# First requests for w_in at 120 partitions each, the last 8 partitions by a request of their own

## The chip, the cores and the metric

One Trainium2 chip; the kernel runs on one of its cores. The metric is the device time of one execution in microseconds, the median of several runs. Before the change it is 368.2 us, median of 3 runs (367.98 to 368.25).

## The reference

Two blocks in a row. The first is a gated linear attention that steps through the sequence (4 batches, 8 heads, 768 steps, head size 48); its output is laid out as 3072 tokens by 384 columns. The second multiplies the tokens by w_in (384 x 1024), applies a softmax-weighted unit with a layer norm, and multiplies by w_out (1024 x 384):

```python
for t in range(S):
    state = alpha[:, :, t, :, None] * state + np.einsum('bhd,bhe->bhde', k[:, :, t], v[:, :, t])
    y[:, :, t] = np.einsum('bhd,bhde->bhe', q[:, :, t], state)
...
h = x @ w_in
e = np.exp(h - np.max(h, axis=-1, keepdims=True))
solu = h * e / (np.sum(e, axis=-1, keepdims=True) + 1e-09)
mu = np.mean(solu, axis=-1, keepdims=True)
var = np.mean((solu - mu) ** 2, axis=-1, keepdims=True)
return ((solu - mu) / np.sqrt(var + 1e-06) * g_ln) @ w_out
```

The inputs are float32, except w_in and w_out: they are float32 arrays times a double, and so reach the kernel as 64-bit floats.

## The kernel before, in words

The sequence is worked in six groups of 128 steps (G = 6), each for all four batches (B = 4), so a group is 512 tokens. For each group the attention is computed in chunk form: decay scans on VectorE (DVE), scores and outputs on TensorE (PE), masks on DVE; then `up` multiplies the tokens by w_in in eight slices of 128 columns (f = 0 to 7, each three matmuls over the 384 rows, which the profile shows as six records) and `down` multiplies by w_out. The order of instructions is written out by hand (`tc.manual_schedule()`): every engine works through its instructions in program order. For group 0 that order is plain code (from line 668 on), for the later groups a table of steps.

The weights come as 64-bit floats and are made into float32 on the chip. There are eight pieces, `pieces`: numbers 0 to 3 are w_in, 256 of its 1024 columns each, numbers 4 to 7 are w_out, 256 of its 1024 rows each. `fetch(i, slot, n)` (line 567) asks for piece i, or for n pieces that follow each other in one go, into a slot of the tile `room`. A w_in piece is requested in three DMA requests, one for each block of 128 rows of w_in (KC = 3): partition p takes row p of the block, 2 KB of it (4 KB with n = 2). `bit(i, k)` (L616 to L630) are five DVE instructions that turn the raw words in `room` into float32 in w_in or w_out; `in_range(i)` (L598 and L601) are two ScalarE (ACT) instructions that read the same words and note whether any is out of range.

What the change and the steps around it touch, in program order:

- SyncE (SP) issues the loads: alpha, k, q (`load_first`), v (`load_v`, L176), then `fetch(0, 3)`, `fetch(1, 4)` and `fetch(2, 1, 2)` at L578: nine requests for w_in, of 256 KB each for pieces 0 and 1 and 512 KB for pieces 2 and 3 together. The next request of SP is that of `fetch(4, 3)` for w_out; it needs slot 3 again, so it waits until piece 0 has been read by L628 and L598.
- Each request signals its end on a semaphore. Eight semaphores are used in turn for all requests of SP and ACT (numbers 101 and 104 to 110 in the trace), and a request waits until the one eight before it has landed.
- DVE: the last masks of the scores (`masked`, L289), then `bits(0)`, the copy `g_col` (L642), `bits(1)`, and then the steps of pieces 2 to 7, spread over the eight slices of group 0 between the products of L409.
- PE: `read_values` (L333), `keys_back` (L303), then `up_mm` (L394). Its h(0) and h(1) need piece 0, h(2) and h(3) piece 1, h(4) and h(5) piece 2, h(6) and h(7) piece 3. h has two PSUM buffers, so h(f) also waits until ACT (L408) and DVE (L409) have read h(f - 2).
- ACT: `keys_back`'s copies, `in_range(0)`, and for each slice the exponential (L408), a step of `in_range` for a later piece (for f = 0 the first of piece 2) and the square (L412).

At the end each engine reads a flag and branches past a general path that isn't taken (L1422); after that SP waits for the eight DMA semaphores one after the other, and all engines meet (L1449).

Of the kernel before, what the change touches and what calls it, by code (L numbers as in the profile page):

```python
# [11 lines left out]
U32 = mybir.dt.uint32  # L12
# [4 lines left out]
P = 128  # L17
# [15 lines left out]
def fast_path(ctx, tc, q, k, v, alpha, moe_w_in, moe_w_out, moe_g_ln, out):  # L33
# [12 lines left out]
    nc = tc.nc  # L46
# [8 lines left out]
    KC = DM // P  # L55
# [117 lines left out]
    def load_v(g):  # L173
        t = slice(g * P, (g + 1) * P)
        for b in range(B):
            nc.sync.dma_start(out=held(vn, b), in_=v[b, :, t, :].rearrange("h p d -> p h d"))  # L176
# [147 lines left out]
    parts = []  # L324
# [231 lines left out]
    float64 = moe_w_in.dtype != FP  # L556
# [7 lines left out]

    raws = {}

    def fetch(i, slot, n=1):

        kind, f = pieces[i]
        w = n * F // (2 if kind else KC)  # L570
        raw = room[:, 1536 * slot : 1536 * (slot + n)].bitcast(U32).rearrange("p (c f w) -> p c f w", f=w, w=2)
        if kind:
            parts = [(slice(0, P), c, moe_w_out[(f + c) * P : (f + c + 1) * P, :]) for c in range(2)]
        else:
            parts = [(slice(0, P), c, moe_w_in[c * P : (c + 1) * P, f * P : f * P + w]) for c in range(KC)]
        for rows, c, src in parts:
            if float64:
                nc.sync.dma_start(out=raw[rows, c].rearrange("p f w -> p (f w)"), in_=src.bitcast(U32))  # L578
            else:
                dst = w_out[rows, f + c, 0:DM] if kind else w_in[rows, c, f * P : f * P + w]  # L580
                nc.sync.dma_start(out=dst, in_=src)
        for m in range(n):
            raws[i + m] = raw[:, :, w // n * m : w // n * (m + 1)]
# [100 lines left out]
    nc.gpsimd.memset(state, 0.0)  # L684
    nc.gpsimd.memset(kg, 0.0)
    load_v(0)
    fetch(0, 3)
    fetch(1, 4)
    fetch(2, 1, 2)
    nc.vector.memset(ones, 1.0)  # L690
    nc.vector.memset(small_ones, 1.0 / 32)
    nc.vector.memset(mhalf, -0.5)
# [24 lines left out]
    for i in (0, 2, 1):  # L717
        if i == 1:
# [3 lines left out]
            out=qe[:, :, 0:P] if i == 2 else qv[:, part, 0:P], in0=t[i], in1=aT[:, part, 1:SW], op=ALU.mult  # L722
# [199 lines left out]
    for g in range(1, G + 1):  # L922
# [10 lines left out]
        for s in range(FC):  # L933
# [18 lines left out]
            if todo:  # L952
                n, half = todo.pop(0)
# [18 lines left out]
    parts = [N * 3, G * 2, G * NB] + [len(pieces)] * 2  # L972
# [5 lines left out]
    def compare(out, x, bound, op):  # L978
# [6 lines left out]
        out=chunks[:, :, 2], in0=sums[:, :, 2], scalar=0.25, in1=sums[:, :, 3], op0=ALU.mult, op1=ALU.is_le  # L985
# [6 lines left out]
    else:  # L992
# [9 lines left out]
        out=bad, in0=all_ok[0:1, 0:1], scalar1=float(P * ends[-1]), scalar2=None, op0=ALU.is_lt  # L1002
# [415 lines left out]
def kernel(tc, *args):  # L1418

    with ExitStack() as ctx:  # L1420
        taken = fast_path(ctx, tc, *args)
    with tc.If(taken > 0):  # L1422
        general_path(tc, *args)
# [30 lines left out]
```

## Time and profile before

| what | value |
|---|---|
| median of 3 runs | 368.2 us (367.98 to 368.25) |
| the profiled execution's own time | 367.97 us |
| its span, first to last instruction | 366.2 us |
| PE busy | 357.8 us (98%) |
| DVE, ACT, POOL busy | 245.0, 146.4, 132.2 us |
| granted TensorE clock | 1.00 |
| w_in requests: count, KB each, us to landing | 6 of 256 KB, 6.1; 3 of 512 KB, 8.0 |

A line of the profile's timeline gives the start in us, how long, the engine (a q marks its sequencer, as for DMA issues), the line of the kernel, the operation, what it writes and reads, the shape and how many were merged; square brackets give idle time of the engine before it and what ended it. The profile is one execution; 367.97 less 366.2 us lie around its span.

### The profile page before, as it was taken

The numbers are of one execution on the slowest core, as the hardware profiler recorded it, in microseconds if no ns is written. First come the engines' busy times: TensorE is split into PE (matmuls) and PEld (weight loads), VectorE is DVE, ScalarE is ACT, GpSimd is POOL, SyncE is SP. The second block draws the span as 40 slices with busy tenths as digits, with TensorE's granted clock in tenths as the row PEclk, the third lists the DMA queues.
The fourth block names the chain that finished last, engine by engine and source line by source line (L and its number), as shares of the span: only waits on it lengthen the run. The fifth ranks groups of instructions, "written<-read, shape, count | busy, mean of one in ns | idle before, by whom it ended". The sixth has DMA issues, their size and how long they took to land. (4 is left out here: it accounts for less than half of the span.)

```text
span 366.2 us, 10036 instructions
## 1 busy us (share of the span) xinstructions
PE 357.8 (98%) x4341; PEld 215.0 (59%) x4341; DVE 245.0 (67%) x375; ACT 146.4 (40%) x260; POOL 132.2 (36%) x129
## 2 busy tenths in 40 slices
PE   8899999999999999999999999999999999999994
PEld 8784355666755566566575456475556565555552
DVE  0999989979998797936675935766946314345420
ACT  3647878182645262252521252431241132222110
POOL 7020000004449963774133764232773121233300
PEclk9999999999999999999999999999999999999999
DMA  9995995326196409463035354004041000000011
GB/s 180 183 338 152 204 309 124 88 67 159 50 234 141 109 21 180 85 152 94 21 92 112 83 121 126 3 25 88 21 107 55 0 25 0 24 21 22 23 47 51
DMA packets 72871, 36.06 MB, mean 98 GB/s; under 512 B 48232, under 2 KB 70000, under 8 KB 72816
## 3 DMA queue, kind: packets, MB, share of 16 engines
q1 hardware_dynamic: 71792, 34.39, 39.8%
q10 hardware_dynamic: 1024, 0.92, 0.8%
q8 instruction: 36, 0.59, 0.7%
q14 instruction: 19, 0.16, 0.2%
HBM read 25.30 MB, written 4.72 MB: 82 GB/s over the span
## 5 line engine op out<-in xcount | busy, mean ns | idle before, releaser
L507 PE MATMUL o<-w_out,room 128*128 128x385 f32 x384 | 134.0, 492 | 0.0
L394 PE MATMUL h<-x,w_in 128*128 128x512 f32 x288 | 131.7, 597 | 0.5 <-DVE g_col L642 0.5
L507 PEld LDWEIGHTS o<-w_out,room 128*128 128x128 f32 x384 | 71.0, 189 | 54.7 <-issue 13.1
L394 PEld LDWEIGHTS h<-x,w_in 128*128 128x128 f32 x288 | 53.2, 189 | 58.6 <-issue 48.5
L409 DVE TENSOR_TENSOR room<-h,e 128x512 f32<-128x512 f32 x40 | 27.5, 689 | 72.9 <-ACT e L408 72.9
L408 ACT ACTIVATE e<-h 128x512 f32<-128x512 f32 x40 | 24.0, 599 | 100.2 <-PE h L394 100.2
L427 POOL TENSOR_TENSOR p<-p,e 128x512 f32<-128x512 f32 x30 | 43.7, 1458 | 20.0 <-ACT e L408 19.9
L412 ACT ACTIVATE u<-room 128x512 f32<-128x512 f32 x40 | 25.2, 630 | 38.3 <-DVE room L409 38.3
L546 POOL TENSOR_TENSOR r<-sums,mhalf 128x1 f32<-128x1 f32 x20 | 14.8, 741 | 69.7 <-DVE sums L537 69.4
L289 DVE TENSOR_TENSOR sT<-a,mask 128x512 f32<-128x512 f32 x43 | 26.7, 681 | 8.0 <-PE a L278 7.9
L204 DVE TENSOR_TENSOR_SCAN hT<-aT,unit 128x516 f32<-128x516 f32 x18 | 24.4, 1399 | 7.6 <-ACT aT L703 7.5
L204 DVE TENSOR_TENSOR_SCAN aT<-aT,seed 128x516 f32<-128x516 f32 x18 | 27.4, 1551 | 0.2
L225 POOL TENSOR_TENSOR kT<-kT,hT 128x1024 f32<-128x1024 f32 (+1 forms) x8 | 14.2, 1800 | 32.7 <-DVE kT L179 32.7
L427 DVE TENSOR_TENSOR p<-p,u 128x512 f32<-128x512 f32 x30 | 22.5, 749 | 5.1 <-ACT u L412 5.1
L278 PEld LDWEIGHTS a<-qv,kT 32*128 32x128 f32 x704 | 21.4, 186 | 7.0 <-issue 2.6
L278 PE MATMUL a<-qv,kT 32*128 32x128 f32 x704 | 23.9, 278 | 0.4 <-POOL qv L253 0.3
L212 POOL COPY fend<-hT 128x12 f32<-128x12 f32 x6 | 3.1, 509 | 55.9 <-DVE hT L204 55.9
L333 PE MATMUL y<-sT,vn 128*32 128x128 f32 x768 | 22.6, 273 | 0.2 <-DVE sT L289 0.2
L333 PEld LDWEIGHTS y<-sT,vn 128*32 128x32 f32 x768 | 20.7, 110 | 1.6 <-issue 1.0
L196 ACT ACTIVATE sq<-an,mone 128x1536 uint8<-128x1536 f32 x12 | 18.9, 1572 | 0.2
L548 ACT ACTIVATE o_sb<-o,r 128x384 f32<-128x384 f32 x16 | 9.3, 582 | 18.5 <-POOL r L546 18.5
L261 POOL TENSOR_TENSOR state<-state,lot 128x384 f32<-128x384 f32 x10 | 8.8, 903 | 13.1 <-DMA lot<-qv 13.1
(148 smaller groups left out, 374.3 us busy)
## 6 DMA issues: line engine op xcount, KB each, us to landing
vn<-in_v_dram SPq DMA_DIRECT2D x24, 192.0 KB, 4.7
an<-in_alpha_dram SPq DMA_DIRECT2D x20, 192.0 KB, 4.1
out_dram<-o_sb SPq DMA_DIRECT2D x20, 192.0 KB, 1.9
room<-in_moe_w_out_dram SPq DMA_DIRECT2D x8, 384.0 KB, 5.5
kn<-in_k_dram SPq DMA_DIRECT2D x16, 192.0 KB, 5.6
qn<-in_q_dram SPq DMA_DIRECT2D x16, 192.0 KB, 4.1
lot<-qe SPq DMA_DIRECT2D x40, 64.5 KB, 2.1
lot<-qv SPq DMA_DIRECT2D x20, 129.0 KB, 2.4
```

The lines of the kernel that those rows point to most:

```text
L196: nc.scalar.activation(out=sq, in_=x, func=AF.Relu, scale=sign, bias=mone, accum_out=over[:, g, i : i + 1])
L204: nc.vector.tensor_tensor_scan(out=o, data0=a, data1=s, initial=1.0, op0=ALU.mult, op1=ALU.add)
L278: nc.tensor.matmul(a[b][:, i], lhsT=kT[quarter(b), kb], rhs=qv[quarter(b), qb, 0:P], start=not last and not i, stop=bool(last), tile_posit ...
L289: nc.vector.tensor_tensor(out=sT[:, b, half * NP : half * NP + NP], in0=a[b], in1=mask[:, None, :].to_broadcast([P, NP, P]), op=ALU.mult,)
L333: nc.tensor.matmul(y_bank(b)[quarter(r), a], lhsT=lhsT, rhs=rhs, start=(b, r) not in begun, stop=stop, tile_position=(row, 32 * r), skip_g ...
L394: nc.tensor.matmul(h, lhsT=w_in[:, a, f * P : (f + 1) * P], rhs=d["x"][:, a].rearrange("p b t -> p (b t)"), start=(a == 0), stop=(a == KC ...
L408: nc.scalar.activation(out=e, in_=h, func=AF.Exp)
L409: nc.vector.tensor_tensor(out=u, in0=h, in1=e, op=ALU.mult)
L412: nc.scalar.activation(out=u2, in_=u, func=AF.Square)
L427: eng.tensor_tensor(out=p, in0=d[0][i] if f == 1 else p, in1=d[f][i], op=ALU.add)
L507: nc.tensor.matmul(d["o"][:, 0 : DM + 1], lhsT=u_of(g, f)[:, b * P : b * P + P], rhs=w_out[:, f], start=(f == 0), stop=(f == FC - 1), skip ...
L546: nc.gpsimd.tensor_tensor(out=r, in0=s[:, 3:4], in1=mhalf, op=ALU.pow)
```

## The change

`fetch` gets an argument `apart`, 0 unless given. The three fetches of w_in ahead of group 0 give 8. Their requests for the three blocks of rows then take partitions 0 to 119 alone, and one request ahead of them takes partitions 120 to 127 of all three blocks (24 rows of 2 KB, or of 4 KB for pieces 2 and 3). The nine requests become twelve. The bytes and where they land are the same. In the changed kernel's order of instructions all engines but SP have the same instructions in the same order; DVE and ACT wait for four semaphores in place of three before they first read a group of pieces.

```diff
-    def fetch(i, slot, n=1):
+    def fetch(i, slot, n=1, apart=0):
...
-            parts = [(slice(0, P), c, moe_w_in[c * P : (c + 1) * P, f * P : f * P + w]) for c in range(KC)]
+            parts = [
+                (slice(0, P - apart), c, moe_w_in[c * P : (c + 1) * P - apart, f * P : f * P + w]) for c in range(KC)
+            ]
+            if apart and float64:
+                nc.sync.dma_start(
+                    out=raw[P - apart : P].rearrange("p c f w -> p c (f w)"),
+                    in_=moe_w_in.rearrange("(c p) f -> p c f", c=KC)[P - apart : P, :, f * P : f * P + w].bitcast(U32),
+                )
+            elif apart:
+                parts += [
+                    (slice(P - apart, P), c, moe_w_in[(c + 1) * P - apart : (c + 1) * P, f * P : f * P + w])
+                    for c in range(KC)
+                ]
         for rows, c, src in parts:
...
-    fetch(0, 3)
-    fetch(1, 4)
-    fetch(2, 1, 2)
+    fetch(0, 3, 1, 8)
+    fetch(1, 4, 1, 8)
+    fetch(2, 1, 2, 8)
```

## The prediction

> **What bounds the kernel now.** I first read the groups and the stage sums, to find the engine that sets the end. From the first matmul of the second block to TensorE's last work the sum over one window (start:end, length, busy time of PE with its instruction count, of PEld, DVE, ACT, POOL) is:
>
> ```profile
> 28.39:361.50 333.11, 332.54 (x3748) 192.27 (x3748) 225.41 (x345) 131.93 (x237) 122.69 (x113) 1.00 0.37 88
> ```
>
> PE is busy for 332.54 of 333.11 us at the full granted clock. All that an edit at the start can change is when this block begins, or a new hole in it. So I read PE's timeline (start, length, what, count, idle time before it):
>
> ```profile
> 28.39 2.81 PE L394 MATMUL h<-x,w_in 128*128 128x512 f32 x6 [0.46 <-DVE g_col L642]
> ...
> 32.63 10.57 PE L394 MATMUL h<-x,w_in 128*128 128x512 f32 x24
> ```
>
> The six records at 28.39 are h(0). It waited for DVE; the 24 at 32.63 are h(1) to h(4), six each at 10.57/24 = 0.44 us, so h(3) starts at 32.63 + 12 x 0.44 = 37.9. What DVE did before them:
>
> ```profile
> 23.31 0.68 DVE L289 TENSOR_TENSOR sT<-a_o,mask 128x512 f32<-128x512 f32 x1
> 23.91 0.76 DVE L616 TENSOR_SCALAR lot<-room 128x768 uint32<-128x768 uint32 x1
> 24.70 0.96 DVE L620 SCALAR_TENSOR_TENSOR lot<-room,lot 128x768 uint32<-128x768 uint32 x1
> 25.70 0.56 DVE L624 TENSOR_SCALAR lot<-lot 128x768 uint32<-128x768 uint32 x1
> 26.29 0.96 DVE L628 SCALAR_TENSOR_TENSOR lot<-room,lot 128x768 f32<-128x768 uint32 x1
> 27.28 0.96 DVE L630 TENSOR_TENSOR w_in<-lot 128x768 f32<-128x768 f32 x1
> 28.16 0.16 DVE L642 TENSOR_SCALAR g_col<-tp_g 128x8 f32<-128x8 f32 x1
> 28.23 0.55 DVE L616 TENSOR_SCALAR lot<-room 128x768 uint32<-128x768 uint32 x1
> ...
> 32.95 0.94 DVE L616 TENSOR_SCALAR lot<-room 128x768 uint32<-128x768 uint32 x1
> ```
>
> L616 to L630 turn the raw bits of piece 0 into w_in, with no idle time in brackets anywhere. L616 begins at 23.91, before the mask of L289 is over (23.31 + 0.68 = 23.99); masks follow each other at the same 0.60. So DVE came to piece 0 in its turn and did not wait for the transfer. It takes piece 1 at 28.23 and piece 2 at 32.95. The transfers, from SP's timeline and the DMA view (KB each, us to landing) of the third request alone:
>
> ```profile
> 16.32 4.83 SPq L578 DMA_DIRECT2D room<-in_moe_w_in_dram  x9
> 29.70 0.80 SPq L578 DMA_DIRECT2D room<-in_moe_w_out_dram  x2
> ```
>
> ```profile
> room<-in_moe_w_in_dram SPq DMA_DIRECT2D x1, 256.0 KB, 6.1
> ```
>
> That request, the last of piece 0, was issued at 17.46 and landed at 23.52: 0.39 us ahead of L616. The trace counts a landing in sixteen steps. Fifteen were there at 22.30, the sixteenth 1.22 later; one 16 KB packet of the instruction queue began at 20.99 and took 0.95. So one DMA engine of the sixteen is late. Pieces 2 and 3, which share requests, had fifteen steps of their second request at 27.09 and were whole at 29.54.
>
> [...] The trace has one request of 8 rows, g_rows at L675: one jump, then eight separate steps[...]; none has 120. [...] the four 192 KB requests to 32 partitions each[...] at 202 to 205 us landed 0.83 us apart, 237 GB/s, while 384 KB to 128 partitions (w_out, 48 to 51 us) took 0.98, 401 GB/s; their rows are shorter (768 B against 3 KB)[...]. [...]
>
> **The change, part by part.** The engines' pace first: fifteen steps of the first request were in at 20.75 and of the third at 22.30, sixteen rows of 2 KB per engine, 0.097 us a row. Piece 0 is 24 rows, 2.33 us, so they began it at about 19.97.
>
> - [...] If it is the late one, piece 0 no longer waits for 23.52. Worth nothing on the path: DVE is at the mask until 23.91.
> - Added: three requests of 8 partitions, ahead of their groups, on eight engines: three rows of 2 KB each for pieces 0 and 1, three of 4 KB for 2 and 3. Lower bound: three rows at 0.097, 0.3 us. Upper: [...]0.9 us, and 1.8 for the wide one. I take the upper[...].
> - Changed: nine requests of 128 become nine of 120, eight rows to an engine as before. Lower bound 0.097 a row. [...] I take 0.097 for the forecast, as the engines already land spread over some 0.8 us (20.78 to 21.59 for the second request)[...].
> - Landing, from these: piece 0 at 19.97 + 0.9 + 2.33 = 23.2 (22.6 with the lower bound), under 23.91 less 0.10 from a landing to its reader (49.45 to 49.55 in the trace), that is 23.81. Pieces 2 and 3 at 19.97 + 3.6 + 96 x 0.097 = 32.9, beside DVE's 32.95; ACT's L598 wants them at 31.73, but had 1.06 us idle ahead of its next L408 (35.51). Nothing reaches PE. The cover is thin: 0.6 us at piece 0, and at pieces 2 and 3 the 0.8 us from the end of L409 of f = 1 (36.39 + 0.68 = 37.07) to h(3) at 37.9.
> - SP: three more issues at the median 0.44 us, 1.3 us. SP holds eight requests at a time, one per semaphore; the ninth waits for the first, now also the tenth to twelfth for the second to fourth, so the last goes out when piece 0 is in, at 23.2 to 24.5. A landing there took 4.8 us (29.70 to 34.47), so 29.3 at the latest, ahead of the engines' own 32.9. Behind them on SP only the w_out request of 29.70 is queued, and that waits for L628 and L598 of piece 0. Nothing on POOL moves. DVE and ACT wait for one semaphore more per piece, ahead of an instruction whose engine is still busy: nothing.
> - The end: three more requests move the last output from the seventh of the eight DMA semaphores to the second. SP looks at them one after another, 0.068 us each (364.21, 364.28), so five more looks follow the last landing: 0.34 us. Covered: SP then stood 0.55 us for ACT, whose branch ended at 362.75 and whose next instruction came at 365.28. Cover gone, it costs the 0.34.
>
> The sum is 0: the profiled execution's 366.2 us of span and 1.8 around it, 367.97, stay. The median of the runs is 368.2, 0.2 more; some of that may be piece 0 landing later than in the profile, so I forecast 368.1.
>
> **The rivals.** *The eight engines and the ports come too late* (slower): [...] It decides at piece 0 from (23.81 - 19.97 - 0.9)/24 = 0.122 us a row, and at pieces 2 and 3 from a landing at about 33.8 (32.95 + 0.8). [...]DVE 2.5 late, L409 ends at 39.6, and h(3) starts 1.7 late: 368.1 + 1.7 = 369.8. [...] For it: the 237 GB/s of 32-partition requests. Against: the spread landings.
>
> [...](the change doesn't do what it says): then 1.2 us stays and piece 0 lands at 23.2 + 1.2 = 24.4, 0.6 over: 368.7. The trace doesn't number the engine.
>
> *Piece 0 binds in the timed runs* (faster): if it is about 1 us later there than in the profile, the whole of it comes back, 367.1. Against: the profiled execution is as fast as the fastest of the runs, 367.98.
>
> **How the numbers follow.** Cover holds, 368.1: 0.45. Late engine stays, 368.7: 0.07. Ports, 369.8 (369.0 to 372.4): 0.38. Piece 0 binding, 367.1: 0.10. A measurement of this kernel can tell about 0.2%, 0.7 us, from no change: same is the first two, 0.52, slower 0.38, faster 0.10. The forecast's own range is 367.8 to 368.7; the one given reaches to 367.6 and, leaving out the upper third of the port case, to 370.6.
>
> **What would show it.** Right: h(0) at 28.39 again, no idle time in brackets at L616, no hole at h(3). The landing steps of piece 0 end together at 22.6 to 23.2[...]. Rows per request: 0.78 us between requests means 0.097[...]. Wrong: a DMA wait at L616 for 23.91 or 32.95, or PE idle before L394 at h(3); or, at the end, SP's last wait no longer for ACT.

## The result, and the profile after

The changed kernel takes 371.9 us, median of 9 runs (368.58 to 373.73); the kernel before, on the same chip, 368.25 (367.98 to 369.9, 9 runs). The ratio is 1.0083 with a 95% interval of 1.0058 to 1.0109: slower by 0.8%, about 3.1 us. The forecast was 368.1, and 371.9 lies above the range's upper end of 370.6. The changed kernel's runs spread over 5 us, those of before over 2. The execution that was profiled is the fastest of the nine (368.58 us, span 366.7), so it shows the change's small costs and not the typical one.

What it shows first: TensorE's window has no new holes, and its busy time is that of before (columns: window, length, busy us and count of PE, PEld, DVE, ACT, POOL; clock, DMA share, GB/s).

```profile
28.39:361.50 333.11, 332.48 (x3748) 192.32 (x3748) 225.26 (x346) 131.62 (x238) 122.59 (x113) 1.00 0.38 91
```

h(0) comes 0.31 us later (28.39 before), and h(1) to h(4) take 10.70 us in place of 10.57, in PE's timeline:

```profile
28.70 2.81 PE L394 MATMUL h<-x,w_in 128*128 128x512 f32 x6 [0.58 <-ACT kg L310]
31.44 1.57 PE L371 MATMUL kv<-vn,kg 128*32 128x48 f32 x128
32.94 10.70 PE L394 MATMUL h<-x,w_in 128*128 128x512 f32 x24
```

In DVE's timeline (L616 has become L628) both reads of raw words, which had no bracket before, now wait: 0.48 us for piece 0, and 0.69 for piece 2, at 34.03 in place of 32.95.

```profile
24.41 0.57 DVE L628 TENSOR_SCALAR lot<-room 128x768 uint32<-128x768 uint32 x1 [0.48 <-issue]
...
34.03 0.95 DVE L628 TENSOR_SCALAR lot<-room 128x768 uint32<-128x768 uint32 x1 [0.69 <-issue]
```

Here "issue" only says that the profile found no releaser for DVE. ACT, which reads the same words (L598 is now L610), names it:

```profile
34.09 0.91 ACT L610 ACTIVATE sq<-room 128x768 f32<-128x768 f32 x1 [1.95 <-DMA room<-in_moe_w_in_dram]
```

The landing steps agree: of the fifteen that the last request of piece 0 counts, fourteen were there at 23.20, the last at 24.33; pieces 2 and 3 were whole at 33.95. The end is as forecast: SP's last wait is still for ACT, so the added looks at semaphores are covered.

```profile
SPq L1461 <- ACTq L1434: 0.4, 1, 0.4
```

The packets show the pace. By the middle one of those that started from 24 to 28 us, a 4 KB packet took 159 ns before and 285 after; one of 2 KB from 20 to 24 us took 84 before and 101 after. So late data are seen, but here they cost 0.5 us of span. Where the other 2 to 3 us of the median are, this profile doesn't tell.

### The profile page after: what moved, and what is told of

It reads as the page before. It is cut to its first block, busy times and chain, and to the rows that moved or that the text cites. A ratio compares the mean times of both kernels' runs of the same rounds, so it can differ in the third digit from the quotient of the medians.

```text
span 366.7 us, 10043 instructions
## 1 busy us (share of the span) xinstructions
PE 357.9 (98%) x4341; PEld 214.8 (59%) x4341; DVE 244.5 (67%) x375; ACT 145.9 (40%) x260; POOL 132.1 (36%) x129
## 5 line engine op out<-in xcount | busy, mean ns | idle before, releaser
L409 DVE TENSOR_TENSOR room<-h,e 128x512 f32<-128x512 f32 x40 | 27.5, 689 | 73.4 <-ACT e L408 73.4
L225 POOL TENSOR_TENSOR kT<-kT,hT 128x1024 f32<-128x1024 f32 (+1 forms) x8 | 14.2, 1801 | 32.9 <-DVE kT L179 32.9
L333 PE MATMUL y<-sT,vn 128*32 128x128 f32 x768 | 22.8, 274 | 0.2 <-DVE sT L289 0.2
L333 PEld LDWEIGHTS y<-sT,vn 128*32 128x32 f32 x768 | 20.7, 110 | 1.9 <-issue 1.3
```

Source lines behind the costliest of these rows:

```text
L333: nc.tensor.matmul(y_bank(b)[quarter(r), a], lhsT=lhsT, rhs=rhs, start=(b, r) not in begun, stop=stop, tile_position=(row, 32 * r), skip_g ...
L409: nc.vector.tensor_tensor(out=u, in0=h, in1=e, op=ALU.mult)
```

## The experiments

My theory at this point: the split requests run slower, their rows come late, and DVE, ACT and so PE wait for the late data. Rivals: the twelve requests themselves (more of them, on eight semaphores), the 8-partition requests, and something that hits only some executions. In the expectations the first is the port theory, after a guess at the reason; no trace here shows a port. Their fifteen and eight engines are read from landing steps: fifteen for a request of 120 partitions, eight for one of 8 (first profile after).

| kernel | median us (range, runs) | ratio to before (95%) |
|---|---|---|
| changed kernel again | 370.92 (368.57 to 373.46, 9) | 1.0076 (1.0052 to 1.0101) |
| only piece 0's requests split | 368.66 (368.2 to 369.59, 12) | 1.0018 (1.001 to 1.0027) |
| only those of pieces 2 and 3 split | 372.77 (371.31 to 374.11, 6) | 1.0121 (1.0098 to 1.0144) |
| split 96 and 32 | 370.47 (369.43 to 373.97, 6) | 1.0084 (1.0053 to 1.0114) |
| twelve requests, all of 128 partitions | 368.28 (367.72 to 369.41, 22) | 1.0 (0.9992 to 1.0008) |
| changed, shorter first warm-up | 372.95 (370.14 to 375.62, 6) | 1.013 (1.0084 to 1.0177) |
| before, shorter first warm-up | 370.2 (369.98 to 373.68, 6) | 1.0055 (1.0042 to 1.0068) |
| changed, no second warm-up | 369.2 (367.97 to 370.76, 14) | 1.0029 (1.0018 to 1.004) |
| before, no second warm-up | 368.4 (367.83 to 369.58, 13) | 1.0008 (0.9999 to 1.0017) |

### The changed kernel again

No edit.

> The changed kernel once more, unchanged, for a profile of one more of its executions: the profiled one (368.58 us) was the fastest of nine, the median was 371.9. Port theory[...]: the 480 KB requests of pieces 2 and 3 take 2.0 to 2.6 us each, in place of 1.3 us for 512 KB before, and the later pieces 2 and 3 land (33.9 us in the profile, up to 38), the longer the execution: a hole of 1 to 4 us in TensorE's work before or in h(1) to h(4). Queue theory (the last three requests go out too late because only eight may be under way): their issue times, 21.4, 23.3 and 24.3 us in the profile, are later by as much as the execution is longer. Late-engine theory: the time follows the landing of piece 0 alone, and h(0) starts 3 us later.

The profile fell on an execution of 373.46 us (span 371.7), 5.5 us of span more than before. PE's timeline:

```profile
28.46 2.81 PE L394 MATMUL h<-x,w_in 128*128 128x512 f32 x6 [0.33 <-ACT kg L305]
31.21 0.28 PE L371 MATMUL kv<-vn,kg 128*32 128x48 f32 x5
32.02 1.55 PE L371 MATMUL kv<-vn,kg 128*32 128x48 f32 x123 [0.54 <-issue]
33.51 2.41 PE L394 MATMUL h<-x,w_in 128*128 128x512 f32 x5
38.77 10.01 PE L394 MATMUL h<-x,w_in 128*128 128x512 f32 x19 [2.85 <-issue]
```

h(0) is only 0.07 us late here. But PE stops twice where it never stopped before: 0.54 us after five records of kv, and 2.85 us after five of the six records of h(1). A wait in the middle of one h is odd: its x and w_in had been read by the five records ahead. And neither wait has a releaser; PE's table of waits for 20 to 340 us:

```profile
PE h L394 <- issue: 2.9, 1, 2.9
PE kv L371 <- issue: 0.5, 1, 0.5
```

The other engines' stall is the effect and not the cause: ACT's exponential waits for PE (and DVE's L409 for that). In ACT's timeline:

```profile
39.76 0.60 ACT L408 ACTIVATE sT<-h 128x512 f32<-128x512 f32 x1 [2.77 <-PE h L394]
```

What can be missing there is instructions. Counting all of PE's records (products, weight loads and a few semaphore instructions), the two holes lie at counts 1217 and 1473, just 256 apart. One instruction queue has packets of 16 KB. The profile doesn't name their engine, but 36 of them, 9216 instructions if each brings the 256 that lie between the holes, fit only PE with its 8740 records; the next, DVE, has 456. They began at 20.99, 27.46, 32.44 and 35.97 us before, at 20.89, 29.45, 36.02 and 40.52 here. The packet at 29.45 took 1.24 us and PE resumed at 32.02; that at 36.02 took 1.26 and PE resumed at 38.77, 1.3 and 1.5 us after the packet's end (1.3 to 1.6 in all the profiles with such a hole). From these counts and times I take it that PE's instructions come in blocks of 256, one 16 KB packet each, and that PE stood at the ends of two blocks until the next was in. The profile doesn't name such a wait; this is an inference.

After the long hole the records show PE's granted clock at 0.5 from 38.87 to 42.28 us. The windows (columns as above) hold the whole loss; the first is the kernel before, the second this execution:

```profile
28.00:55.00 27.00, 26.61 (x268) 12.82 (x272) 25.48 (x36) 21.21 (x44) 0.00 (x0) 1.00 0.90 224
```

```profile
28.00:55.00 27.00, 23.28 (x187) 10.15 (x186) 20.73 (x29) 17.22 (x37) 0.00 (x0) 0.94 0.85 213
55.00:100.00 45.00, 45.00 (x703) 28.94 (x705) 41.85 (x63) 25.36 (x48) 4.60 (x10) 1.00 0.53 126
```

The starts of h(0) to h(4) against before (28.39, 32.63, 35.31, 37.88, 40.46) give the bill: late by 0.07 at h(0), 0.88 at h(1) (the first hole), 4.20 at h(2) (the second), 5.59 at h(3) (the half clock) and 5.58 at h(4): the span's difference. Pieces 2 and 3 had landed at 34.56, 0.6 us later than in the execution of 368.58. The half clock is not in every long run: of these nine, only the three at 372.34 and above have a mean clock of 0.993 or 0.994, the other six 0.996 to 1.000; so 370 to 372 us are reached without it.

This makes a second theory, of instructions: slow rows hold up the packet with PE's next block.

### One part of the change alone

Only piece 0's requests split:

```diff
-    fetch(1, 4, 1, 8)
-    fetch(2, 1, 2, 8)
+    fetch(1, 4)
+    fetch(2, 1, 2)
```

> 120 and 8 partitions for piece 0 alone; pieces 1 to 3 by whole requests as before. Port theory: piece 0 lands at 24.0 to 25.0 us and costs 0.2 to 1.2 us through h(0), but pieces 2 and 3 are back to the pace of 1.3 us a request and land by 31: 368.4 to 369.3 us. Late-engine theory: all of the cost is here, 371 to 372 us. Queue theory: one request more, the last goes out after the second of piece 0 has landed: 368.2 us.

Only those of pieces 2 and 3:

```diff
-    fetch(0, 3, 1, 8)
-    fetch(1, 4, 1, 8)
+    fetch(0, 3)
+    fetch(1, 4)
```

> 120 and 8 partitions for pieces 2 and 3 alone. Port theory: most of the cost is here, because their three 480 KB requests take 2.0 to 2.6 us each and land 2 to 4 us after the 32.95 us at which VectorE wants them: 370 to 372 us; piece 0 as before, h(0) at 28.4. Queue theory: the last request goes out when the second of piece 0 has landed, at 21.6 us, as the ninth did before at 20.8: 368.2 to 369. Late-engine theory: 368.2.

Piece 0 alone costs 0.2%: in its profile (368.65 us, span 366.9) it lands at 24.55, h(0) starts at 28.91, 0.52 late, after DVE, which read piece 0 at 24.63 in place of 23.91. A hole of 0.29 us at record 961, well ahead of h(0), is no part of that, for PE then waits 0.37 us for DVE; no hole follows; 4 KB packets take 162 ns from 24 to 28 us, near the old pace. So the cost doesn't follow piece 0, as a late engine would have it. Pieces 2 and 3 alone cost 1.2%, no less than the whole change (0.76%; the two intervals overlap a little). PE's timeline in the profiled execution of 373.72 us:

```profile
29.43 2.81 PE L394 MATMUL h<-x,w_in 128*128 128x512 f32 x6 [1.12 <-DVE g_col L654]
32.18 0.28 PE L371 MATMUL kv<-vn,kg 128*32 128x48 f32 x5
32.72 1.55 PE L371 MATMUL kv<-vn,kg 128*32 128x48 f32 x123 [0.27 <-issue]
34.20 2.41 PE L394 MATMUL h<-x,w_in 128*128 128x512 f32 x5
38.64 6.58 PE L394 MATMUL h<-x,w_in 128*128 128x512 f32 x11 [2.03 <-issue]
```

The same holes at the same records (1217 and 1473), and the half clock again, 39.12 to 42.54. Piece 0, whose requests are the old ones, lands at 25.12 in place of 23.52, and h(0) comes 1.04 late; why its last step is later here is open.

### Which requests are slow

The first kernel here makes only the nine requests of 120 partitions: the last 8 rows of each block of w_in are left out, and zeros stand in their place.

```diff
-            if apart and float64:
...
+    nc.gpsimd.memset(room[96:P, 1536:7680], 0.0)
```

> The nine requests of 120 partitions without the three of 8: the last 8 rows of each block of 128 rows of w_in are left out (zeros in their place, written by GpSimd early on), so nothing runs on eight engines alone and there are nine requests, as before. Port theory: a 240 KB request still takes 0.95 to 1.2 us and a 480 KB one 2.0 to 2.6; without the 3.6 us of the small requests pieces 2 and 3 land at 30 to 34.5 us: 368.2 to 369.0 us, with the slow pace to be seen. Eight-engine theory (the small requests cost it all, those for 120 partitions run at 0.78 and 1.35 us as those for 128): pieces 2 and 3 land at 28.5 to 29.5, 368.2 us, with the old pace. Queue theory: as before, 368.2.

It took 1206.82 us, which says nothing: zeros are out of the range that `in_range` looks for, and the general path ran. Its first 40 us can be read: 2 KB packets of 102 ns from 20 to 24 us and 134 from 24 to 28, 4 KB packets of 266, piece 0 at 25.26 us, a hole of 1.13 us at record 961, and in PE's timeline the holes at 1217 and 1473:

```profile
32.79 1.55 PE L371 MATMUL kv<-vn,kg 128*32 128x48 f32 x123 [0.70 <-issue]
34.27 2.41 PE L394 MATMUL h<-x,w_in 128*128 128x512 f32 x5
38.71 4.00 PE L394 MATMUL h<-x,w_in 128*128 128x512 f32 x5 [2.03 <-issue]
```

So the slow pace is there without any 8-partition request. Next, a split into 96 and 32 partitions, with no 8-partition request either:

```diff
-    fetch(0, 3, 1, 8)
-    fetch(1, 4, 1, 8)
-    fetch(2, 1, 2, 8)
+    fetch(0, 3, 1, 32)
+    fetch(1, 4, 1, 32)
+    fetch(2, 1, 2, 32)
```

> The changed kernel with 96 and 32 partitions in place of 120 and 8: twelve requests again[...]. Port theory[...]: packets of 2 KB take over 100 ns in the median in place of 84, those of 4 KB over 200 in place of 159, and the time is 369 to 373 us. Fifteen-and-eight-engine theory (what costs is that one engine has nothing to do and eight have more): packets of 84 and 159 ns, 368.1 us.

And twelve requests that all keep 128 partitions, the third block in two halves of its columns:

```diff
+            if float64 and not kind and c == 2:
+                for x in range(2):
+                    y = slice(w // 2 * x, w // 2 * (x + 1))
+                    nc.sync.dma_start(out=raw[rows, c, y].rearrange("p f w -> p (f w)"), in_=src[:, y].bitcast(U32))
```

> Twelve requests in three groups of four as in the changed kernel, all of 128 partitions: the third block of rows of each group comes in two requests of half the columns. Queue theory (with twelve requests the last three wait for the first to land): the last requests go out at 21.5 to 24 us and the time is 369 us or more. Port theory: 84 ns for 2 KB as before, pieces 2 and 3 landed by 30 us, 368.1 us.

The split of 96 and 32 is as slow as the change (1.0084): 4 KB packets at 293 ns from 24 to 28 us, pieces 2 and 3 at 34.62, and in PE's timeline of its fastest execution (369.43) a hole at record 1473:

```profile
33.30 2.41 PE L394 MATMUL h<-x,w_in 128*128 128x512 f32 x5
36.55 8.31 PE L394 MATMUL h<-x,w_in 128*128 128x512 f32 x19 [0.84 <-issue]
```

Twelve whole requests cost nothing (1.0, within 0.1%): 84 and 159 ns as before, pieces 2 and 3 at 29.17. So the pace is slow neither for the number of requests, nor for the semaphores, nor for the 8-partition requests: in these runs it is slow where w_in's requests take fewer than all 128 partitions. The reason isn't shown: what these runs show is the pace alone.

### Moving the block ends: the first warm-up

If PE lacks instructions, the holes must stay at their counts and move to other work when records are taken out ahead of them. The first warm-up (products that nobody reads) shrinks from 14 to 6, 32 records fewer; the second kernel does the same to the kernel before.

```diff
-    warm(14)
+    warm(6)
```

> The changed kernel with 6 warm-up matmuls at the start in place of 14, so that TensorE's program is 32 records shorter ahead of everything else. Instruction theory (in the slow executions TensorE ran out of instructions: its 16 KB blocks end at records 1217 and 1473, 256 apart, where it stood 0.5 and 2.9 us for nothing that the profile names, because the packet with the next block started late behind w_in's rows): the blocks now end 32 records later in the program, the second in h(4) in place of h(1), some 7 us later, when the packet has long come: the long hole and the halved clock after it are gone, 368.3 to 369.5 us. Data theory (h(1) or h(2) waited for pieces 2 and 3 through ScalarE or VectorE): the hole stays in h(1) and the time at 370.5 to 372.

> The kernel before with 6 warm-up matmuls in place of 14, the control for the run with the changed one. Either theory: 368.1 us and no hole; should fewer warm-up matmuls leave TensorE's clock low at the start, both runs show it, with the start of h(0) later by up to 2 us.

The long hole left h(1), as only the instruction theory says; but it didn't go away. In PE's timeline of the changed kernel with the shorter warm-up (371.57 us) it lies in kv, again at record 1217:

```profile
32.38 0.45 PE L371 MATMUL kv<-vn,kg 128*32 128x48 f32 x21
34.82 1.38 PE L371 MATMUL kv<-vn,kg 128*32 128x48 f32 x107 [1.99 <-issue]
```

Its packet began at 32.00. The expected time was missed, and so was the control's: the kernel before with the same edit loses 0.55%, 1.9 us. Part of that need have nothing to do with block ends, as the control's expectation had feared; how much, isn't shown. Its profile shows the full clock from 10.61 us, where it began at 4.71 in the kernel before, 58 records of tp_a took 3.41 us in place of 1.83, and PE came to the values of L333 at 23.40 in place of 22.02. The changed kernel with this edit starts as late (full clock from 10.08 us, L333 at 23.29). The control's profiled execution is also the longest of its six (373.68 us; the others take 369.98 to 370.31) and so not the typical one. It has a hole of its own at record 961, in the values of L333, with the packet at 25.03 in place of 20.99 and the half clock after it:

```profile
24.23 1.07 PE L333 MATMUL y<-sT,vn 128*32 128x128 f32 x30 [0.20 <-DVE sT L289]
27.44 4.27 PE L333 MATMUL y<-sT,vn 128*32 128x128 f32 x86 [2.13 <-issue]
```

So PE can stand at a block's end with the old requests, too, here for 2.13 us. But this edit delayed the start as well as moving the block ends; a cleaner one was needed.

### Moving the block ends without a slow start: the second warm-up

The second warm-up has 16 records and comes at 13.29 us, when the clock has long been full (from 4.71 us). Without it every later block ends 16 records further on: in kv that is some 0.1 us, but at record 1473 it is 16 records of h.

```diff
-    warm(4, ps_a, "a1")
```

> The changed kernel without the second warm-up (16 TensorE records fewer ahead of kv, nothing else; its product is not read). Instruction theory: the block end at record 1473, at 35.9 us between h(1) and h(2), comes 16 matmuls of h later (16 x 0.446 = 7.1 us, at about 43 us), while the 16 KB packet still lands at about 36 us: no long hole there, no half clock after it, at most 0.5 us at record 1217 in kv; time 368.3 to 369.5 us. Theory of late data (late rows of pieces 0, 2 and 3 are the cost): the rows land as before, so the hole of 2 to 3 us stays between h(1) and h(3), and the time stays at 370.5 to 372.

> Control: the kernel before without the second warm-up. Both theories: no hole, 368.0 to 368.4 us. If it is slower by more than 0.3%, taking the warm-up away costs something by itself, and the run with the change has to be read against this one.

Both times came out as the instruction theory says. The shift was misjudged: a product and its weight load are two records, so 16 records are eight products, and record 1473 comes at 38.8 us, not at 43; that is still late enough. PE's timeline of the changed kernel without it (profiled execution 368.57 us):

```profile
28.79 2.81 PE L394 MATMUL h<-x,w_in 128*128 128x512 f32 x6 [0.79 <-DVE g_col L654]
31.54 1.57 PE L371 MATMUL kv<-vn,kg 128*32 128x48 f32 x128
33.03 5.42 PE L394 MATMUL h<-x,w_in 128*128 128x512 f32 x12
38.68 5.42 PE L394 MATMUL h<-x,w_in 128*128 128x512 f32 x12 [0.23 <-DVE room L409]
```

No hole without a releaser is left, though the rows are as late as ever: 4 KB packets of 279 ns, pieces 2 and 3 at 34.41, and DVE waits for them:

```profile
34.49 0.95 DVE L628 TENSOR_SCALAR lot<-room 128x768 uint32<-128x768 uint32 x1 [1.05 <-issue]
```

The packets that the two block ends need began at 27.20 and 33.42; the second, 1.28 us long, was in at 34.7, some 4 us ahead of record 1473. None of the 14 runs is over 370.76, where seven of nine of the changed kernel had been over 371 in the first comparison, and four of nine in the second. What is left is 0.8 us against its control (369.2 to 368.4), and the two profiled spans differ by 0.6: that is about what the late data cost in this pair, 0.33 at h(0) (28.79 to 28.46) and 0.40 more at h(3), of which DVE's L409 is the releaser for 0.23. So of the change's 2.8 to 3.1 us (0.76 to 0.83%), some 0.8 are late data, and the other 2 are PE's instructions.

## Why the prediction was wrong

The step that failed is "Nothing reaches PE". The prediction followed late data alone to TensorE; the runs show some 0.8 us of late data, from a pace that it took too fast, and some 2 us of late instructions, a path that it put at nothing by not naming it. Step by step, as the prediction put them:

- *The late engine: piece 0 no longer waits for it, worth nothing.* Half right: worth nothing, but piece 0 still had a late one. The idea was that requests of 120 partitions leave one of the sixteen engines without rows, and that this is the late one. The trace numbers no engine: it counts fifteen steps for each request of 120 partitions and eight for each of 8, and a step as one engine's share is my reading of it; which engines a request takes isn't shown. One step of the fifteen still came last, at 24.33, and the eight of the 8-partition request of piece 1, asked for behind piece 0, were all in at 23.63. If an engine works through its requests in order, which isn't shown, the late one is none of those eight. A packet of the instruction queue began at 21.03 here, as one had at 20.99, and took 1.03 us, so what the prediction called the likely cause may still have made an engine late. The rival of the late engine gave 24.4 for piece 0 and was right on the number; which engine was late isn't shown.
- *Added: 0.9 us for each 8-partition request, 1.8 for the wide one.* Both were estimates of mine that no trace shows. The first request was whole at 19.58, so nothing of it stands in the way of piece 0; the price was too high and did no harm.
- *Changed: 0.097 us a row.* This term was mis-sized. From the first block's fourteenth step to the third's, 21.30 to 23.20, sixteen rows took 1.90 us: 0.119 a row, where the prediction took its lower bound. For pieces 2 and 3 the steps at 29.50, 31.58 and 33.88 give 2.08 and 2.30 for eight rows of 4 KB, 0.130 to 0.144 per 2 KB. The argument for 0.097, that the engines already land apart (20.78 to 21.59), didn't hold.
- *Landing: piece 0 at 23.2, pieces 2 and 3 at 32.9.* Fourteen of the fifteen steps made 23.20 by luck: a pace too fast and a first request too dear cancelled; pieces 2 and 3 came at 33.95 to 34.56. The threshold of 33.8 to h(3) was well placed: at 34.41, in the kernel without the second warm-up, h(3) was 0.40 later.
- *Nothing reaches PE.* This failed, by 0.8 us through the data and by 2 through the instructions. The prediction named what each queue holds behind the requests, SP's and POOL's, but not the instruction queue, though it had shown one of its packets, at 20.99 us, as the likely cause of the late engine. That PE was busy throughout said nothing of how near its next block came to being late. In the kernel before, the packet that record 1473 needs began at 32.44, took 0.92 and was in at 33.36; with the 1.3 us or more that PE took after a packet in every hole, PE could go on at 34.7 at the earliest, and it passed the record at 34.88. The cover was 0.2 us at most (and none at record 961: its packet was in at 21.94, and PE went on at 23.25). In the execution of 373.46 us the packet came 3.6 us later (36.02), while PE passed record 1217 only 0.8 later (32.02 for 31.18).
- *SP and the end: covered.* Right. SP's twelve issues ended at 24.7, and its last wait is for ACT.
- *The rival of the ports, 369.8.* Nearest to the time, with 0.38. A slow pace is what was measured, 0.119 to 0.144 us a row; the ports that it is named for, and so the sizes it gave for DVE's delay (2.5 us) and for its own range (369.0 to 372.4), were my estimate and are not shown. Its path to the end, through DVE's L409 to h(3), exists but is worth 0.4 us, not 1.7. Most of the loss took another path, so that its time is near the measured one is partly luck.
- *Piece 0 binding in the timed runs, 367.1.* Not put to the test: piece 0 landed at 24.33, later than before and not earlier.

What stays open: why the requests of fewer than 128 partitions were slower was not measured by itself. That they hold up the instruction packet is argued from its times. The 16 KB packet for record 1473 began at most 1.3 us after PE passed record 1217 in the five profiles with whole requests for pieces 2 and 3, and 1.8 to 4.0 us after in six of the seven without; by what order an engine serves the two queues isn't shown. The seventh is the first profile of the changed kernel: its packets came at 26.65 and 31.28, with no hole at the same slow pace. Why an execution falls on one side or the other is not known.

## What to carry to other kernels

Before splitting a transfer for the sake of one late engine, measure the pace of the split itself: in the seven profiles where pieces 2 and 3 came by requests of fewer than 128 partitions, the middle 4 KB packet from 24 to 28 us took 266 to 407 ns, in the others 159 to 162, and the number of requests did not matter. Count the instruction queue among a transfer's neighbours: on a bound engine, a wait without a releaser, in the middle of identical work and at counts 256 apart, pointed to a late block of instructions here, and the cover of the next one is worth computing like that of any buffer. Taking out a few unneeded instructions moves such an end: without the second warm-up the change costs 0.2% against its control in place of 0.8. But look at what else they did: without part of the first warm-up the kernel before lost 0.55%, in part to a clock that came up 5.9 us later.

## What the runs showed of the hardware that was not expected

- A 2 KB packet took 84 ns in the kernel before and 133 (the middle one from 24 to 28 us) in the changed kernel's second profile; a 4 KB one 159 and 271. A split of 96 and 32 gave 132 and 293.
- TensorE stood at counts that lie 256 records apart (961, 1217, 1473) for 0.27 to 2.85 us in seven of the twelve profiles, and went on 1.3 to 1.6 us after the end of a 16 KB packet.
- After holes of 2.03, 2.13 and 2.85 us the granted clock was 0.5 for 3.41 us, after those of 1.99 and 0.84 it was not. The clock fell 34.13 us after full clock had begun in three profiles and 17.07 after in the fourth, ten and five times 3.413; in the first profiles before and after the full clock lasted 361.81 us, 106 times that. From these figures I estimate a fixed row of windows of 3.413 us. Counted so, each hole with a fall lies whole inside one such window; the hole of 1.99 us crosses a window's end at 33.97 us and leaves 1.14 us idle in one and 0.85 in the next. In the first 360 us of all twelve profiles the clock fell after every window with 2.03 us or more idle and after none with 1.37 or less; there was none between. A limit on a hole's own length, between 1.99 and 2.03 us, would fit these holes as well.
